# A spectral mixer beside a gated MLP: the column stage streams its tiles from DRAM, and the second half of the tokens runs as block products

## The chip, the cores and the metric

The kernel runs on one core of a Trainium2 chip. A core has TensorE (matrix products into PSUM), VectorE and ScalarE (elementwise work, and all reads of PSUM), GpSimd and SyncE (here mostly issuers of DMAs), and 16 DMA engines between DRAM and SBUF. The metric is device time in microseconds (us); lower is better.

## The reference

Two branches read the same 2048 x 576 input `x`, and a gate per token mixes them:

```python
g = sigmoid((x * gate_w).sum(-1, keepdims=True))
a = irfft2(rfft2(x) * (w_r + 1j * w_i))              # over 2048 tokens and 576 features
b = (gelu(x @ w_gate) * (x @ w_up)) @ w_down         # 576 -> 4608 -> 576, tanh form of gelu
out = g * a + (1 - g) * b
```

Everything is float32.

## The kernel before

**Precision.** Each float32 operand of a matmul is split into a high part of 12 bits and a remainder; a product is three matmuls: high x high, remainder x high, high x remainder. ScalarE makes the high copies, VectorE the remainders. The 576 features are 512 plus 64. Of the last 64 the high part and remainder are stacked along the rows, so that one matmul multiplies several of the three terms at once.

**The MLP.** The 2048 tokens are two halves of 1024, and a half has two token blocks of 512. The 4608 hidden features are 36 tiles of 128, two tiles to a block, so 18 blocks in a half. A *plain* block (`normal` L1510, `hidden` L892, `chain` L853) computes gate and up for two tiles and two token blocks: 2 x 2 x 2 chains of 14 matmuls. A *block product* (`products` L1300) gets the same from seven products instead of eight (Strassen's scheme in Winograd's form): features and tokens are halved, and seven pairs of sums of input parts (`a11`, `a12`, `s2`, `s3`, `s1`, `a22`, `s4`) and of weight parts are multiplied. `seven` (L1285) runs one such product, for gate and for up, with 7 matmuls each: six for two feature tiles of 128 and one, the seventh, for the stacked last 32 features of each feature half. `FIRST = (2, 6)` (L32): in half 0 the first 2 blocks are plain and 16 are block products, in half 1 it is 6 and 12. Each block then has 96 output matmuls of 288 columns (`down` L960, `down_mm` L935), eight groups of 12. ScalarE scales each group by 1 - g into one of four buffers `stg` (L977), and GpSimd issues a DMA that adds it to an accumulator `yd` in DRAM (L958).

**Weights of a block product.** `load` (L1237) fetches four quarters `r11, r21, r12, r22` of 128 x 768 (384 KB); the last 256 columns are the stacked tail. `prep` (L1256) is called three products ahead: VectorE takes differences of quarters (L1269), two gaps later ScalarE copies the high part (L240, and the tail with a mask at L1276), two further gaps on VectorE takes the remainder (L1279). The slots are four, used in turn. The remainders of 18 down weights are stored to DRAM in half 0 (L836) and fetched in half 1 (L829).

**Input operands of half 1.** The split inputs of the seven products of half 0 lie in `til`, `xhi`, `xlo` and `xtl`. Half 1's are made in half 0 and kept in DRAM as `kept` and `four_d` (`other_operands` L1143). During half 1's six plain blocks `til` holds the spectral tiles; after it the operands are fetched from `kept`.

**The spectral branch** is a generator (`spectral` L705): gates and forward row transforms of each half (`forward_rows` L531, `send_away` L580, which writes 16 tiles of 128 x 580 to `away` in DRAM), the column stage (`columns` L252), the last tile butterflies (`last_tiles` L450), and for each half inverse rows (`inverse_rows` L628) and the addition of g times the result to `yd` (`adds` L669). In `columns` all 16 tiles lie in `til`. For each tile: `product(0)`, a 128 x 128 complex transform in 6 matmuls on TensorE (L305), a filter on VectorE, `product(1)` back, and copies into the tile. Filter tables (`load_ww` L275, two pairs) and transform matrices (`load_cc` L271, two of each kind) are loaded two tiles or five steps ahead. `corner` (L280) regroups two quarters of a tile with DMAs of 72.5 KB.

**The order of work is written out by hand.** The program is built in TensorE's order. After every chain half, `seven` or `down`, `gap` (L742) runs: it counts, starts what was set for that count with `at(n, ...)` (n gaps later), and lets the generator go on while it has credit. Each matmul gives credit at RATE = 1.08 times its charged time (`tick` L731: 0.2265 us for 512 columns, 0.131 for 288), and each piece of VectorE work takes its charge away, the block products' own work too. `yield None` in the generator ends its turn for this gap. A block product with its output groups has 22 gaps. Each engine, and each queue of DMA issues (SyncE's `SPq`, GpSimd's, ScalarE's), takes its instructions strictly in this order, so an instruction that waits holds those behind it. In the last block, whatever the generator still has is drained with TensorE idle, ahead of the final reads of `yd` (`load_last` L997).

## Time and profile before

| | |
|---|---|
| runs | 1323.91, 1324.33, 1324.39 us; median 1324.33 |
| profiled execution | span 1323.4 us from first to last instruction; the page gives no other time for it, so 0.9 us of the median lie outside |
| TensorE busy, clock | 1317.2 us (100%), 7294 matmuls, 1.00 of full speed |
| VectorE / ScalarE / GpSimd busy | 1163.2 (88%) / 871.8 (66%) / 274.5 us (21%) |
| DMA | 247.57 MB, mean 187 GB/s; accumulating queue 45.2%, sync queue 34.1% of 16 engines' time |

Busy times of an engine are the sum of its instructions. Matmuls are pipelined, so a single matmul's duration (392 ns for 512 columns) is longer than the time it adds. A DMA share is the mean busy share of 16 engines by the time of their packets, and can pass 1 where packets overlap.

### The profile page before, as it was taken

How to read it: one execution, taken by the hardware profiler on the slowest of the kernel's cores; microseconds unless marked ns; L12 is line 12 of the kernel's file. 1: busy time of each engine (PE TensorE's matmuls, PEld its weight loads, DVE VectorE, ACT ScalarE, POOL GpSimd, SP SyncE). 2: the span in 40 equal slices, each digit the busy share in tenths (PEclk: the TensorE clock that was granted, in tenths of full speed). 3: DMA queues.
4: the chain of work that ended last, by engine and by line, in shares of the span. 5: the costliest groups of instructions: out<-in, count | busy, mean ns of one | idle time of the engine just before them, and what ended most of it. 6: DMA issues, size and time to landing. Idle time of an engine off the chain costs nothing.

```text
span 1323.4 us, 20232 instructions
## 1 busy us (share of the span) xinstructions
PE 1317.2 (100%) x7294; PEld 1166.3 (88%) x7294; DVE 1163.2 (88%) x1654; ACT 871.8 (66%) x1583; POOL 274.5 (21%) x347
## 2 busy tenths in 40 slices
PE   9999999999999999999999999999999999999998
PEld 7888888888888888888888898888888888888888
DVE  7789999978999997976889889799999879999854
ACT  5676765665657557787688888547675676676562
POOL 0011121221212212122302231211222242222331
PEclk9999999999999999999999999999999999999999
DMA  9346776797677777999989998787777897766897
GB/s 352 139 116 130 131 135 136 158 267 167 146 153 139 151 156 183 278 237 280 284 251 247 219 210 206 124 279 194 153 150 148 202 232 163 135 141 131 182 195 181
DMA packets 109221, 247.57 MB, mean 187 GB/s; under 512 B 12864, under 2 KB 18624, under 8 KB 107328
## 3 DMA queue, kind: packets, MB, share of 16 engines
q0 software_dynamic: 46560, 96.82, 45.2%
q1 hardware_dynamic: 62128, 149.01, 34.1%
q8 instruction: 57, 0.93, 0.3%
q10 hardware_dynamic: 432, 0.44, 0.1%
q14 instruction: 44, 0.36, 0.1%
HBM read 133.88 MB, written 109.95 MB: 184 GB/s over the span
## 4 chain that ended last, share of the span: by engine, by line
PE 96%; DVE 2%; DMA 1%; ACT 0%; issue 0%; SPq 0%; DVEq 0%; ACTq 0%
PE pdn L945 33%; PE pgu L1292 20%; PE px L1292 20%; PE pgu L1294 3%; PE px L1294 3%; PE pgu L861 3%; PE pgu L862 3%; PE pgu L863 3%; DMA til<-away 1%; PE pdn L305 1%; PE px L305 1%; PE px L861 1%; PE px L862 1%; PE px L863 1%; PE pgu L867 1%; PE pgu L868 1%
## 5 line engine op out<-in xcount | busy, mean ns | idle before, releaser
L958 POOL DMA_DIRECT2D yd<-stg x264 | 227.0, 865 | 937.7 <-ACT stg L977 864.3
L977 ACT ACTIVATE stg<-pdn,omg 128x576 f32<-128x576 f32 x276 | 204.4, 742 | 318.1 <-PE pdn L945 197.2
L945 PE MATMUL pdn<-dn,hb 128*128 128x288 f32 x1572 | 230.3, 294 | 0.0
L945 PEld LDWEIGHTS pdn<-dn,hb 128*128 128x128 f32 x1572 | 221.5, 188 | 8.9 <-ACT stg L977 0.4
L1279 DVE TENSOR_TENSOR gub<-low,gub 128x768 fp32r<-128x768 f32 x124 | 118.2, 954 | 9.7 <-ACT gub L1276 7.3
L1292 PE MATMUL pgu<-xhi,gub 128*128 128x512 f32 x392 | 121.6, 392 | 0.0
L240 ACT ACTIVATE gub<-low 128x512 fp32r<-128x512 f32 (+2 forms) x147 | 97.8, 666 | 23.0 <-DVE low L1269 14.5
L945 PEld LDWEIGHTS pdn<-dn,ext 128*128 128x128 f32 x672 | 100.8, 188 | 8.0
L1292 PE MATMUL pgu<-til,gub 128*128 128x512 f32 x420 | 107.5, 391 | 0.0
L945 PE MATMUL pdn<-dn,gub 128*128 128x288 f32 x672 | 106.5, 294 | 0.0
L945 PE MATMUL pdn<-dn,ext 128*128 128x288 f32 x672 | 106.5, 294 | 0.0
L945 PEld LDWEIGHTS pdn<-dn,gub 128*128 128x128 f32 x672 | 95.0, 188 | 0.0
L1292 PEld LDWEIGHTS pgu<-til,gub 128*128 128x128 f32 x420 | 76.9, 188 | 14.8 <-DVE gub L1279 0.3
L1292 PE MATMUL px<-xhi,gub 128*128 128x512 f32 x280 | 86.9, 391 | 0.0
L1292 PE MATMUL px<-til,gub 128*128 128x512 f32 x336 | 85.8, 391 | 0.0
L945 PE MATMUL pdn<-dn,hx 128*128 128x288 f32 x516 | 81.7, 294 | 0.0
L1292 PEld LDWEIGHTS pgu<-xhi,gub 128*128 128x128 f32 x392 | 70.9, 188 | 12.1
L1269 DVE TENSOR_TENSOR low<-low 128x768 f32<-128x768 f32 x81 | 77.2, 954 | 0.8
L1292 PE MATMUL pgu<-xlo,gub 128*128 128x512 f32 x196 | 76.4, 390 | 0.0
L862 PE MATMUL pgu<-xhi,gub 128*128 128x512 f32 x188 | 73.7, 392 | 0.0
L861 PE MATMUL pgu<-xhi,gub 128*128 128x512 f32 x188 | 73.7, 392 | 0.0
L863 PE MATMUL pgu<-xlo,gub 128*128 128x512 f32 x188 | 73.3, 390 | 0.0
(274 smaller groups left out, 2966.6 us busy)
## 6 DMA issues: line engine op xcount, KB each, us to landing
yd<-stg POOLq DMA_DIRECT2D x264, 288.0 KB, 5.0
low<-ws SPq DMA_DIRECT2D x94, 384.0 KB, 4.8
gub<-wd SPq DMA_DIRECT2D x56, 288.0 KB, 3.9
low<-wgu SPq DMA_DIRECT2D x13, 640.0 KB, 8.6
rows<-col POOLq DMA_DIRECT2D x32, 256.0 KB, 6.4
gub<-ws SPq DMA_DIRECT2D x18, 384.0 KB, 5.3
lo<-dn SPq DMA_DIRECT2D x18, 288.0 KB, 2.9
dn<-lo POOLq DMA_DIRECT2D x18, 288.0 KB, 5.4
```

The lines of the kernel that those rows point to most:

```text
L240: act.activation(o, i, AF.Copy)
L305: pe.matmul(v[al][:, :NK], c[:, al, q], two(x)[:, al], start=n == 0, stop=n == 2)
L861: pe.matmul(ps, w[:, 0, k, c], xhi[tb][:, k], start=k == 0, stop=False)
L862: pe.matmul(ps, w[:, 1, k, c], xhi[tb][:, k], start=False, stop=False)
L863: pe.matmul(ps, w[:, 0, k, c], xlo[tb][:, k], start=False, stop=False)
L945: pe.matmul(ps[half], h[:, l, c], d[:, q, half * HD:(half + 1) * HD], start=part == 0 and n == 0, stop=part == 1 and n == 2)
L958: pl.dma_start(yd[u], o, accum_op=ALU.add)
L977: at(n, lambda: put(u, lambda o: act.activation(o.rearrange("p (c k) -> p c k", c=2), v[:, :, 0:HD], AF.Copy, scale=omg[:, u:u + 1]), i == 0))
L1269: vec.tensor_tensor(o, p, q, ALU.subtract)
L1279: vec.tensor_tensor(w[:, 0:5:2], x, f(w[:, 1:4]), ALU.subtract)
L1292: pe.matmul(ps, l, x[:, t], start=first and t == 0 and q == 0, stop=False, skip_group_check=True)
L1294: pe.matmul(ps, w[:, 512 + P * s:512 + P * (s + 1)], xt, start=False, stop=True, skip_group_check=True)
```

## The change

1. `FIRST = 2`: only the first two blocks of half 0 are plain. Half 1 is 18 block products, without plain blocks, without its own plain weights, inputs (`xt[1]`), and without the stored down remainders (`lo`).
2. Tails of weights: a weight quarter is now 128 x 512 (256 KB). The last 64 rows go apart: `tail_piece` loads them for two blocks of four pairs (`PAIRS`), takes the differences for all seven products, splits them once, and stores the result in DRAM (`tails_d`). `prep` then fetches a tail into rows 0 to 95 of its slot with three DMAs of 32 x 256 (32 KB each) on SyncE's queue, 21 a block. The seventh matmul uses 96 rows.
3. All seven operands of half 1 are kept in DRAM (`kept`, 1280 KB each) and fetched with three DMAs each from ScalarE's queue, two gaps after half 0's last use of the same operand (`swap`).
4. The column stage no longer needs `til`: tiles are loaded from `away` four at a time into a part of `rows`, regrouped by four DMAs of 72.5 KB each (`bring`), and results are written to `gone` (`leave`). `product` uses the `pdn` PSUM buffers; the filter tables and the transform matrices have one buffer instead of two. A tile takes 6 steps instead of 5. The stage starts as soon as `other_operands` is done, in half 0, among block products.
5. `inverse_tiles` (instead of `last_tiles`) reads `gone`, does the last twiddles, and writes `home`; `inverse_rows` fetches from `home` and does the final butterfly itself (`arrive`).

The core of the diff:

```diff
-STEP = 5
-FIRST = (2, 6)
+STEP = 6
+FIRST = 2
+PAIRS = ((2, 3, 4, 5), (6, 7, 8, 9), (10, 11, 12, 13), (14, 15, 16, 17), (0, 1))
...
+        gone = dram.tile([P, 16 * SW], F32, name="gone", tag="gone")
+        home = dram.tile([P, 16 * SW], F32, name="home", tag="home")
+        kept = {n: dram.tile([P, 2560], F32, name=f"kept_{n}", tag=f"kept_{n}")
+                for n in ("a11", "a12", "s2", "s3", "s1", "a22", "s4")}
+        tails_d = [dram.tile([3 * P, 7 * 256], F32, name=f"tails{i}", tag=f"tails{i}") for i in range(len(PAIRS))]
...
+            inp = [rows[:, 7 * SW:8 * SW], wtb[:, 2 * SW:3 * SW]]
+            w0, w1 = (wtb[:, SW * i:SW * (i + 1)] for i in range(2))
...
+            def load_g(kb):
+                if kb < 16:
+                    q = SW * (kb // 4 + 4 * (kb % 4))
+                    nc.sync.dma_start(G[kb % 4], away[:, q:q + SW])
...
-                    pl.dma_start(cc(s, kb), a["col"][s, turn[kb]])
+                    for q, o in cc_parts[s]:
+                        pl.dma_start(o, a["col"][s, turn[kb]][:, q:q + o.shape[1]])
 
             def load_ww(kb):
                 if kb < 16:
+                    for c, w in enumerate((w0, w1)):
...
+            def bring(kb):
+                if kb < 16:
+                    o, i = two(inp[kb % 2]), two(G[kb % 4])
                     for c in range(2):
-                        nc.sync.dma_start(ww[kb % 2][c], a["wf"][turn[kb], c])
-
-            def corner(kb, slot, back):
-
-                if not 0 <= kb < 16:
-                    return
-                z, c = two(Z[kb]), cns[slot + kb % 2]
-                if back:
-                    copy(z[0:64, 1], c[0:64])
-                    copy(z[64:128, 0], c[64:128])
-                else:
-                    nc.sync.dma_start(c[0:64], z[64:128, 0])
-                    nc.sync.dma_start(c[64:128], z[0:64, 1])
-
-            def rest_of(l, x, h):
-                vec.tensor_tensor(l, x, f(h), ALU.subtract)
+                        for al in range(2):
+                            nc.sync.dma_start(o[64 * c:64 * c + 64, al], i[64 * al:64 * al + 64, c])
+                    at(4, lambda: load_g(kb + 4))
+
+            def leave(kb):
+                q = SW * (4 * (kb // 4) + kb % 4)
+                o, i = gone[:, q:q + SW], two(out)
+                for c in range(2):
+                    nc.sync.dma_start(o[:, NK * c:NK * (c + 1)].rearrange("(l m) k -> m l k", l=2), i[64 * c:64 * c + 64])
...
-                load_cc(d, kb + 2)
+                at(1, lambda: load_cc(d, kb + 1))
...
+                v = product(0, kb, xh, xl)
+                if was:
+                    copy(yh, vs)
+                yield from step()
...
+                if not new:
+                    bring(kb + 2)
...
+                u = product(1, kb - 1, yh, yl) if was else None
+                vec.tensor_tensor(z, z, w0, ALU.mult)
+                vec.tensor_tensor(vs, vs, w1, ALU.mult)
+                vec.tensor_tensor(z, z, vs, ALU.add)
+                vec.tensor_tensor(vs2[:, 0], zr, zi, ALU.add)
+                vec.tensor_tensor(vs2[:, 1], zr, zi, ALU.subtract)
+                at(3, lambda kb=kb: load_ww(kb + 1))
+                if new:
+                    yield from group(new)
+                    bring(kb + 2)
+                yield from step()
+                if was:
+                    copy(two(out), u[:, :, :NK])
+                    at(1, lambda kb=kb: leave(kb - 1))
...
+            def load(d):
+                if d < 4:
+                    nc.sync.dma_start(places[d % len(places)], gone[:, 4 * SW * d:4 * SW * (d + 1)])
+
+            def store(d, x):
+                nc.sync.dma_start(home.rearrange("p (e d k) -> p d e k", d=4, e=4)[:, d],
+                                  x.rearrange("p (e k) -> p e k", e=4))
...
+            for d in range(4):
+                yield from four(T[d], range(4), sp, 1)
+                if d > 1:
+                    yield from tile_twiddles(T[d - 1], d - 1, LEFT, 1, tmps)
+                if d == 0:
+                    leave(0)
+                else:
+                    tile_copies(T[d], d, LEFT, 1, tmps)
+                    if d > 1:
+                        at(1, lambda d=d: leave(d - 1))
...
+        def arrive(e):
+            B = tmp[:, 0:4 * SW].rearrange("p (t k) -> p t k", t=4)
+            yield from _butterfly(vec, lambda i: B[:, i], lambda i: B[:, i, re], lambda i: B[:, i, im],
+                                  range(4), wtb[:, 0:SW], 1, (0.76, 0.45))
+            yield from moved(lambda t, c: (spread(c, t), batch[:, t % 4, c, 0:KF]),
+                             range(4 * (e % 2), 4 * (e % 2) + 4))
+
+        def fetch(e):
+            nc.sync.dma_start(tmp[:, 0:4 * SW], home[:, 4 * SW * e:4 * SW * (e + 1)])
...
+                fetch(0)
                 yield from waits(4)
-                yield from inverse_stages()
+                yield from arrive(0)
+                at(2, lambda: fetch(1))
+                yield from waits(6)
+                yield from arrive(1)
             else:
-                yield from back_again(1)
-                yield from inverse_stages()
-            while ops.get("phase") != 1:
-                yield None
-            places = [zb[0][:, 1920:1920 + D]] + [mk(f"spare{n}", [D]) for n in range(2)]
+                yield from arrive(3)
+            yield from inverse_stages()
...
-            while not back[0] or count[0] < back[0]:
-                yield None
             yield from columns()
-            yield from last_tiles()
+            yield from inverse_tiles()
...
+        def swap(name):
+            hi, lo, tail = ops[name]
+            for o, q in ((hi, 0), (lo, 1)):
+                act.dma_start(f(o), kept[name][:, 1024 * q:1024 * (q + 1)].rearrange("p (t k) -> p t k", t=2))
+            act.dma_start(f(tail), kept[name][:, 2048:])
...
+            ring = [free_low[:, 0:TB], free_low[:, TB:2 * TB], wtb[:, 2 * TB:3 * TB],
+                    *(tmp[:, TB * i:TB * (i + 1)] for i in range(4)), zb[0][:, 1664:1664 + TB]]
...
+                        at(2, lambda n=n, h=h: nc.sync.dma_start(kept[n][:, 2048:], h))
+                    else:
+                        def store(n=n, i=i, h=h, o=o):
+                            for c, s in ((0, h), (1, o)):
+                                nc.sync.dma_start(kept[n][:, 1024 * c + TB * i:1024 * c + TB * (i + 1)], s)
+                        at(2, store)
...
+        def tail_piece(n):
+
+            def load():
+                for q, o in enumerate((raw_t[:, 0:2], raw_t[:, 3:7:3])):
+                    nc.sync.dma_start(o, a["wt"][n // 2, n % 2, q].rearrange("p (b k) -> p b k", b=2))
+
+            def total():
+                for o, p, q in ((4, 3, 0), (2, 6, 4), (3, 6, 3), (5, 1, 2)):
+                    vec.tensor_tensor(raw_t[:, o], raw_t[:, p], raw_t[:, q], ALU.subtract)
+                credit[0] -= 1.15
+
+            def high():
+                copy(high_t, raw_t)
+
+            def rest():
+                vec.tensor_tensor(fr(raw_t), raw_t, f(high_t), ALU.subtract)
+                credit[0] -= 1.1
+
+            def store():
+                d = tails_d[n // 2].rearrange("(r p) (m c k) -> r p c m k", r=3, m=7, c=2)
+                for r, x in enumerate((high_t, high_t, raw_t)):
+                    nc.sync.dma_start(d[r, :, n % 2], f(x) if r < 2 else x)
+                stored[n // 2] = n % 2
...
+                self.groups = [(0, i) for i in range(FIRST, NBLK)] + [(1, i) for i in range(NBLK)]
...
-                        credit[0] -= 0.95
-
-                w, x = (z.rearrange("p (b k) -> p b k", k=256) for z in (w, x))
+                        credit[0] -= 0.69
+
+                def tail():
+                    n, q = self.tail_at[self.groups[k][1]]
+                    assert stored[n]
+                    d = tails_d[n].rearrange("(r q p) k -> q r p k", r=3, q=4)[q, :, :, 256 * m:256 * (m + 1)]
+                    for r in range(3):
+                        nc.sync.dma_start(f(w[32 * r:32 * r + 32, 512:768]), d[r])
...
-                    copy(w[:, 1:4:2], x[:, 0:3:2])
-                    act.activation(w[:, 2], x[:, 1], AF.Copy, scale=msk[:, 1:2])
+                    copy(v[:, 1:4:2], x)
 
                 def rest_of():
-                    vec.tensor_tensor(w[:, 0:5:2], x, f(w[:, 1:4]), ALU.subtract)
-                    credit[0] -= 1.0
+                    vec.tensor_tensor(v[:, 0:5:4], x, f(v[:, 1:4:2]), ALU.subtract)
+                    credit[0] -= 0.69
...
+                seq(("b", k, m), (lead, total), (lead + c, high), (lead + c, tail), (lead + d, rest_of))
...
-                pe.matmul(ps, w[:, 512 + P * s:512 + P * (s + 1)], xt, start=False, stop=True, skip_group_check=True)
+                pe.matmul(ps, w[0:96, 512 + P * s:512 + P * (s + 1)], xt[0:96], start=False, stop=True,
+                          skip_group_check=True)
...
+            if 0 < k <= 2 * len(PAIRS) - 2:
+                for n, fn in zip((1, 8, 10, 13, 15), tail_piece(k + 1)):
+                    at(n, fn)
...
+                if turn:
+                    assert ops["kept"]
+                    at(2, lambda name=name: swap(name))
...
+        b = Block()
+        for i in range(FIRST):
+            for tb in range(2):
+                normal(i, tb, b)
+        for k in range(len(b.groups)):
+            if k == len(b.groups) - 1:
+                assert ops["half"]
+                for u in range(8):
+                    nc.sync.dma_start(a["y"][u], yd[u])
+            products(b, k)
```

685 lines of the change are left out of this document (268 added, 417 removed).

## The prediction

> **What bounds the kernel now.** I read the page first (busy times, slices, chain), then a table of stretches whose borders come from the chain of waits in order of time, then the waits of TensorE.
>
> ```profile
> span 1323.4 us, 20232 instructions
> ...
> PE 1317.2 (100%) x7294; PEld 1166.3 (88%) x7294; DVE 1163.2 (88%) x1654; ACT 871.8 (66%) x1583; POOL 274.5 (21%) x347
> ...
> PE 96%; DVE 2%; DMA 1%; ACT 0%; issue 0%; SPq 0%; DVEq 0%; ACTq 0%
> ```
> ```profile
> 168.30 3.16 PE pdn L945 x24
> ...
> 203.31 3.16 PE pdn L945 x24
> ...
> 845.05 3.16 PE pdn L945 x24
> ...
> 883.23 3.16 PE pdn L945 x24
> ```
> ```profile
> 0.00:35.00 35.00, 33.55 (x151) 27.84 (x152) 27.71 (x49) 20.91 (x38) 3.11 (x10) 1.00 0.95 351
> 140.00:175.00 35.00, 35.00 (x196) 31.01 (x195) 33.47 (x52) 24.79 (x50) 6.86 (x8) 1.00 0.69 130
> 623.00:658.00 35.00, 35.00 (x207) 31.59 (x206) 28.75 (x47) 22.36 (x35) 11.69 (x15) 1.00 1.07 291
> 655.00:830.00 175.00, 174.30 (x994) 155.90 (x993) 157.14 (x266) 143.22 (x265) 35.29 (x51) 1.00 0.89 226
> 1302.00:1323.40 21.40, 17.36 (x117) 16.35 (x115) 12.02 (x19) 2.55 (x5) 0.28 (x1) 1.00 0.61 183
> ```
> ```profile
> PE px L305 <- DVE rows L293: 0.7, 1, 0.7
> ```
>
> The columns of a stretch are its length, the busy time of TensorE, weight load, VectorE, ScalarE and GpSimd, the granted clock, the DMA share and GB/s. TensorE is busy 1317.2 of 1323.4 us at clock 1.00. Its 6.2 idle us are 1.45 at the start, 4.04 at the end, and 0.70 at one wait early in the column stage. So the time is a count of matmuls, and an edit pays only by removing some or by making TensorE wait.
>
> The 24 output matmuls that close a block return every 35.01 us among block products (168.30 to 203.31) and after 38.18 us where a plain block was done (845.05 to 883.23). Both kinds run 96 output matmuls; a block product has 7 x 2 x 7 = 98 gate/up matmuls, a plain block 2 x 2 x 2 x 14 = 112. So 14 gate/up matmuls are 3.17 us and 12 output matmuls 3.16 / 2 = 1.58, and one product with its output set is 4.75.
>
> **What TensorE loses.** The second half had 6 plain blocks of 18 (FIRST = (2, 6)) and now has none: 6 x (38.18 - 35.01) = **19.0 us off**. The column stage keeps 16 x 2 x 6 = 192 matmuls. The seventh matmul of each group has 96 rows instead of 128; no row of before has such a shape, and its nearest rows are the 128-row ones, which stream 512 columns either way. I take no gain and no loss. The 0.70 us wait was on the split of the first column tile; a new prologue with 11 gaps of waiting replaces it, so **0.7 off**.
>
> **What VectorE and ScalarE gain and lose.**
>
> ```profile
> L1279 DVE TENSOR_TENSOR gub<-low,gub 128x768 fp32r<-128x768 f32 x124 | 118.2, 954 | 9.7 <-ACT gub L1276 7.3 <-PE px L1294 2.3
> L1276 ACT ACTIVATE gub<-low,msk 128x256 fp32r<-128x256 f32 x124 | 61.8, 498 | 0.0
> L1269 DVE TENSOR_TENSOR low<-low 128x768 f32<-128x768 f32 x81 | 77.2, 954 | 0.8
> L1312 DVE TENSOR_TENSOR xraw<-xraw 128x512 f32<-128x512 f32 x56 | 38.4, 686 | 9.6 <-ACT xraw L1316 9.5
> L833 DVE TENSOR_TENSOR dn<-gub,dn 128x576 fp32r<-128x576 f32 x38 | 28.6, 752 | 0.0
> L833 DVE TENSOR_TENSOR gub<-low,gub 128x1280 fp32r<-128x1280 f32 x13 | 19.3, 1487 | 0.2 <-ACT gub L240 0.2
> ```
>
> A block product makes 7 remainders and 4 differences of weights. They shrink from 768 columns (954 ns) to 512 (686): 28 x 11 x 0.954 = 294 us become 34 x 11 x 0.686 = 257. Six more blocks add 24 sums (+16), 12 remainders of plain weights go (12 x 1.487 = -18), the 18 down remainders that were stored and fetched are computed again (18 x 0.752 = +14), and ten tail pieces cost by the planner's charges 2.25 each (+22). VectorE stays near 1160 us, 89% of a shorter span: no new bound. ScalarE sheds the 498 ns copy seven times a block, 3.5 us. All of this lies beside TensorE and is worth nothing while every remainder is ready: a block weight is prepared three products (14.2 us) ahead, finished 4 gaps later (22 gaps to 35.01 us, so 1.59 each), which leaves 8 us.
>
> **What the DMAs gain.**
>
> ```profile
> yd<-stg POOLq DMA_DIRECT2D x264, 288.0 KB, 5.0
> low<-ws SPq DMA_DIRECT2D x94, 384.0 KB, 4.8
> rows<-col POOLq DMA_DIRECT2D x32, 256.0 KB, 6.4
> ...
> low<-wf SPq DMA_DIRECT2D x16, 290.0 KB, 6.4
> ...
> ext<-til SPq DMA_DIRECT2D x48, 72.5 KB, 5.6
> ```
> ```profile
> L289 SPq DMA_DIRECT2D ext<-til x24: 461/467/1459, 647.7 to 821.5; - x24
> ```
>
> The last figure of an issue row is the median time to landing; the other row has the min/median/max ns of one issue on SyncE.
>
> Each block now fetches its tail weights in 21 DMAs of 32 KB, 21 x 0.47 = 10 us of SyncE's queue. They are issued about 3 gaps into a lead of 14 us, so landing in 5.6 us leaves 3 to 4 us for whatever waits ahead of them on SyncE. Bytes per block: 8 x 288 + 4 x 256 + 2 x 288 + 21 x 32 KB = 4.7 MB, 134 GB/s, against 130 measured.
>
> The column stage moves, per tile: filter 580 KB, tile from DRAM 290, regrouping 290, two matrices 512, result 290: 2.0 MB, where before it was 1.4 MB. It is 16 x 6 steps of one gap plus about 19 gaps for the three groups made inside: 115 x 1.59 + 26 us of column matmuls = 209 us, 155 GB/s. Together 290 GB/s for 209 us; before, the stage ran at 226 GB/s and share 0.89.
>
> New waits. The filter tables are single: loaded 3 gaps after the filter, wanted 3 gaps (4.8 us) on, landing 6.4 plus an issue. VectorE stands about 2 us per tile, with block remainders queued behind it; their 8 us hide this until landing nears 11 us. The matrices are single too: product to product is 6 gaps and two products, 11 us, the load is issued one gap in, so 8 to 9 us are there for a landing of 6.4, behind the accumulates on GpSimd's queue. This wait is TensorE's own and nothing hides what exceeds it. Regrouping has 7 gaps, but 4 (6.4 us) right after a group, against 4 issues and 5.6 us: ScalarE is late by about 1 us three times.
>
> **The turn** from half 0 to half 1: 21 DMAs on ScalarE's queue bring 7 x 1280 KB = 9.2 MB in one block, each operand wanted one block later. The last block of half 0 runs from about 592 to 627 us (the closing matmuls at 168.30, 12 periods on), and by the planner's charges the columns start near 586, so they collide. Over the 57 us in which all must land, 57 x 290 GB/s = 16.5 MB + 9.2 = 25.7 MB. Bounds: the fastest stretch above moved 351 GB/s, 20.0 MB in 57 us, so 5.7 MB or 16 us are over; at the 291 of the fastest stretch that had accumulates in it, 9.1 MB or 31 us. Against that stand the four output buffers (4 x 4.75 - 5.0 = 14 us) and the weights, about 11 us of allowance. That gives 5 to 20 us; below nothing is excluded, since no matmul goes. I take the lower end, **+5**, because the stretch at 291 cost TensorE nothing (35.00 of 35.00), though its share was 1.07: a share above 1 counts overlapping packets, and is no wall.
>
> **Sum.** 1323.4 - 19.0 - 0.7 + 5 = 1308.7. The runs' median, 1324.3, lies 0.9 over the profiled span: **1309.6 us**; its own range 1304 (no stall) to 1318.
>
> **Rivals.**
>
> *The DMAs bound the column stage (slower side).* Place: first column product to the landing of the turn's operands and the last tile. Need: 209 us x 290 GB/s + 9.2 = 69.8 MB. At 284 GB/s, the mean of the 70 us in which before's column stage opens (row below), that takes 246 us: 37 more than planned, less 11: +26, 1304.6 + 26 = **1331**. It decides from about 292 GB/s down, where the stall reaches 20 us and eats the gain. For it: no row with accumulates held more than 291, and landing rose there.
>
> ```profile
> DMA packets 9373, 19.87 MB, mean 284 GB/s; under 512 B 1019, under 2 KB 1787, under 8 KB 9368
> ...
> til<-away SPq DMA_DIRECT2D x8, 580.0 KB, 9.7
> yd<-stg POOLq DMA_DIRECT2D x12, 288.0 KB, 7.7
> ```
>
> Against it: in those 70 us TensorE lost 0.7. The Trainium skill (DMA: Bandwidth & Descriptors, Issuing engines are not separate DMA queues) says that DMAs issued from the scalar, sync and gpsimd engines run on the same 16 DMA engines and interleave, so a third queue adds no bandwidth. By that rule the turn pays in full and this rival is the outcome; the rise of the accumulates' landing from 5.0 to 7.7 us beside the sync queue's load agrees with it.
>
> *The spectral chain does not end in time.* The last block drains what is left of it with TensorE idle.
>
> ```profile
> L567 DVE TENSOR_TENSOR rows<-tmp x8: 740/794/854, 1060.9 to 1083.4; 128x289 f32<-128x289 f32 x8
> ```
> ```profile
> 1257.55 0.82 DVE L683 TENSOR_SCALAR gub<-rows,gs 128x576 f32<-128x576 f32 x1
> ```
> ```profile
> 1299.84 7.60 SPq L999 DMA_DIRECT2D stg<-yd  x4
> ```
>
> Before, the last scaling came at 1257.6, 42 us ahead of the final reads (1299.84). A block now leaves the spectral side 1.08 x 34.8 - 17.4 = 20.1 planner units instead of 16.9 to 18.4, so 78.5 units of inverse row stages take about 141 us instead of 154 (1083.4 to the scalings from 1237 on). Adding the stages up (columns 586 to 801, tiles to 863, rows to 1048 and 1251) puts the last scaling near 1272, the final reads at 1281: 9 us of room on a sum uncertain by 20. An overrun of 20 us leaves 12 units to drain: +12 on 1304.6 + 5, **1322**.
>
> *The tails come late.* If SyncE is held 4 us longer than above (a store that waits for VectorE ahead of them), every block pays: 0.1 us per product x 238 = 24 us, **1333**. Against: SyncE has 56 issues x 0.47 = 26 us per 35 us in the column stage, 13 elsewhere, so at most the column stage pays.
>
> **How the numbers follow.** Forecast 0.57, DMA-bound columns 0.26, late chain 0.12, late tails 0.05. A change under 0.2% (2.6 us) can't be told from none. Faster: nearly all of the first, a third of the second (stalls up to 17 us) and half of the third, 0.70; same: 0.08; slower: 0.22. The range starts at the floor, 1304, and reaches past 1331 to 1334, where the rest of the DMA case, about 0.12, and late tails beyond it are left out.
>
> **What would show it.** Right: 7210 matmuls, closing matmuls 35.01 us apart outside the columns, TensorE idle about 11 us, all of the increase between 590 and 800 us, and a DMA share at 1.0 there. TensorE waits named after the matrix loads or the operands' swap show the turn; waits spread over all 16 tiles show the DMA rival; idle TensorE ahead of the final reads shows the late chain; waits of weight loads on tail DMAs in every block the last one. The forecast is wrong if the column stage is stretched by more than 12 us, or if the closing matmuls stand further apart than 35.01 us in the pure block stages.

## The result and the profile after

The changed kernel takes **1388.97 us** (median; 1385.02 to 1389.90) against 1324.31 (1323.91 to 1324.39): ratio 1.0483, 95% interval 1.0468 to 1.0498. It is 64.7 us slower, where 14.7 us faster was forecast. Ratios and intervals use fast executions alone; the only slow one (1360.5 us at a clock of 0.92) belongs to the run g1 below. The profiled execution took 1389.90 us, with this page:

```profile
span 1388.1 us, 21347 instructions
...
PE 1330.7 (96%) x7210; PEld 1168.4 (84%) x7210; DVE 1150.5 (83%) x1814; ACT 802.4 (58%) x1395; POOL 274.8 (20%) x345
...
PEclk9999999999999999998899999999999999999999
```

The 84 matmuls are gone (7294 to 7210), and VectorE is no fuller. But TensorE is idle for 1388.1 - 1330.7 = 57.4 us instead of 6.2, and its fewer matmuls take *more* busy time. The chain of waits in the stage of block products alone tells one reason:

```profile
1001.52 3.18 PE pdn L891 x24
...
1036.83 3.18 PE pdn L891 x24
...
1072.14 3.18 PE pdn L891 x24
```

The closing matmuls stand 35.31 us apart. Before it was 35.01. Over 34 block products 0.30 us each make 10.2 us.

So the 64.7 us are: matmuls -19.0, longer blocks +10.2, idle time 57.4 - 6.2 = +51.2, and the rest of the growth of busy time, 1330.7 - (1317.2 - 19.0 + 10.2) = +22.3. The table of stretches shows where the last two lie (length; busy time of TensorE, weight load, VectorE, ScalarE, GpSimd, each with its number of instructions in brackets; clock, DMA share, GB/s):

```profile
560.00:980.00 420.00, 378.62 (x2030) 329.93 (x2029) 307.87 (x521) 258.92 (x456) 86.59 (x118) 0.96 0.93 242
...
560.00:595.00 35.00, 28.06 (x143) 23.55 (x142) 20.76 (x33) 28.16 (x50) 7.72 (x10) 0.95 0.92 252
630.00:665.00 35.00, 23.74 (x111) 20.30 (x110) 18.84 (x33) 17.36 (x30) 6.29 (x9) 0.85 0.95 277
665.00:700.00 35.00, 27.69 (x147) 24.63 (x146) 22.39 (x38) 18.01 (x32) 5.99 (x8) 0.85 0.97 262
770.00:805.00 35.00, 30.96 (x167) 26.83 (x166) 24.66 (x44) 21.98 (x39) 5.86 (x9) 0.95 0.93 253
980.00:1330.00 350.00, 350.00 (x1928) 309.45 (x1927) 320.83 (x473) 200.21 (x344) 76.68 (x89) 1.00 0.79 155
1330.00:1388.10 58.10, 46.17 (x272) 42.17 (x270) 31.19 (x48) 15.69 (x26) 15.44 (x17) 0.94 0.87 186
```

From 980 to 1330 TensorE is full at clock 1.00. Of the 57.4 idle us 41.4 lie between 560 and 980, worst from 630 to 700, and 11.9 in the last 58. Where TensorE stalls, its granted clock falls too. And these are its waits (us in total, times, longest):

```profile
PE pdn L891 <- ACT stg L923: 27.2, 9, 7.3
PE pdn L891 <- DVE low L956: 8.0, 2, 7.1
PE pgu L1286 <- ACT xraw L235: 7.0, 1, 7.0
PE pdn L307 <- DMA tmp<-col: 2.9, 3, 1.3
```

It hardly ever waits for a DMA itself (the longest group, on the transform matrices, has 2.9 us). It waits for ScalarE to empty the PSUM buffers of the output groups (L923): what was late lies further back.

### The profile page after: what moved, and what is told of

It is laid out like the page before. It is cut to its first block, busy times and chain, and to the rows that moved or that the text cites. A ratio compares the mean times of both kernels' runs of the same rounds, so it can differ in the third digit from the quotient of the medians.

```text
span 1388.1 us, 21347 instructions
## 1 busy us (share of the span) xinstructions
PE 1330.7 (96%) x7210; PEld 1168.4 (84%) x7210; DVE 1150.5 (83%) x1814; ACT 802.4 (58%) x1395; POOL 274.8 (20%) x345
## 5 line engine op out<-in xcount | busy, mean ns | idle before, releaser
L923 ACT ACTIVATE stg<-pdn,omg 128x576 f32<-128x576 f32 x276 | 204.3, 742 | 380.6 <-PE pdn L891 245.2
L891 PE MATMUL pdn<-dn,ext 128*128 128x288 f32 x816 | 134.4, 301 | 22.4 <-ACT stg L923 14.3
L1286 PE MATMUL pgu<-xhi,gub 128*128 128x512 f32 x480 | 152.5, 399 | 1.0 <-DVE gl L1311 1.0
L1286 PE MATMUL pgu<-til,gub 128*128 128x512 f32 x516 | 135.3, 398 | 7.0 <-ACT xraw L235 7.0
L235 ACT ACTIVATE gub<-low 128x512 fp32r<-128x512 f32 (+1 forms) x163 | 100.8, 620 | 31.3 <-DVE low L1257 17.6
L1273 DVE TENSOR_TENSOR gub<-low,gub 128x512 fp32r<-128x512 f32 x151 | 103.4, 684 | 3.4 <-ACT gub L235 3.4
L1286 PE MATMUL pgu<-xlo,gub 128*128 128x512 f32 x240 | 94.7, 395 | 0.0
L1286 PEld LDWEIGHTS px<-til,gub 128*128 128x128 f32 x396 | 72.6, 188 | 14.0
L1286 PEld LDWEIGHTS px<-xhi,gub 128*128 128x128 f32 x344 | 62.2, 188 | 13.1 <-DVE xraw L1328 1.5
L93 DVE TENSOR_TENSOR rows<-rows 128x1280 f32<-128x1280 f32 (+1 forms) x57 | 69.5, 1219 | 0.8
L1288 PE MATMUL pgu<-til,gub 96*128 96x512 f32 x172 | 68.3, 397 | 0.3 <-DMA gub<-tails 0.3
```

Of the source, the lines that this page charges most:

```text
L93: eng.tensor_tensor(o, p, q, op)
L235: act.activation(o, i, AF.Copy)
L891: pe.matmul(ps[half], h[:, l, c], d[:, q, half * HD:(half + 1) * HD], start=part == 0 and n == 0, stop=part == 1 and n == 2)
L923: at(n, lambda: put(u, lambda o: act.activation(o.rearrange("p (c k) -> p c k", c=2), v[:, :, 0:HD], AF.Copy, scale=omg[:, u:u + 1]), i == 0))
L1273: vec.tensor_tensor(v[:, 0:5:4], x, f(v[:, 1:4:2]), ALU.subtract)
L1286: pe.matmul(ps, l, x[:, t], start=first and t == 0 and q == 0, stop=False, skip_group_check=True)
```

## The experiments

Below, 1389 is the changed kernel. Single executions are compared with it, and its own spread over 5 us, so smaller differences are not read; g1 to g3 were timed in three rounds.

### The turn, the tails, the bytes

```diff
 e1_no_turn
-                    at(2, lambda name=name: swap(name))
 e2_tails_once
+                once = [(lead + c, tail)] if 7 * k + m < 4 else []
+                seq(("b", k, m), (lead, total), (lead + c, high), *once, (lead + d, rest_of))
 e3_few_bytes  (swap, load_ww, load_cc)
+                n = SW if kb == 0 else SW // 4
```

> The changed kernel without the 21 fetches of the turn on ScalarE's queue: half 1's block products use half 0's operands, so the second half's MLP is computed from the wrong inputs; everything else stands. Theory T (the turn's 9.2 MB stall the two blocks around it): the worst stretch, 630 to 700 us, where TensorE was busy 51 of 70 us at a clock of 0.85, becomes like its neighbours (64 of 70), about 1365 us. Theory Q (SyncE's queue: the column stage's own fetches stand behind tail fetches that wait for TensorE): no more than 10 us are gained, 1380 or above. Theory B (too many bytes for the DMA engines): 9.2 MB at 270 GB/s are 34 us, so about 1355.

> The changed kernel, where only the first four products fetch a tail into their slot and all later products reuse what lies there: 234 of 238 times three DMAs of 32 KB are gone from SyncE's queue, and the tail rows of the result are wrong. Theory Q: the 351 us in which SyncE's queue stood at these fetches go, the column stage's fetches are issued in time, and the idle 57 us of TensorE shrink to under 25, the clock with them: about 1335 us. Theory T: the stage keeps its stalls, 1385. Theory B: 0.69 MB less per block over some 10 blocks is 7 MB or 25 us: about 1362.

> The changed kernel with the same DMAs in the same order, but the turn's, the filter tables' and the transform matrices' (after the first tile) move a quarter of their columns: about 7 + 12 = 19 MB less between 590 and 890 us, and the operands of half 1 and the filters are wrong. Theory B: 19 MB at 270 GB/s are 70 us of DMA time, so the stalls of the stage are nearly gone, 1335 us or less. Theory Q: the order of the queue is what it was, so at most 15 us are gained, 1375. Theory T says what the run without the turn says, about 1365.

Measured: without the turn **1365.6**, with tails fetched once **1371.4**, with a quarter of the bytes **1356.4**. The turn costs 23 us, as theory T had it, but T alone promised 1385 for the run without tail fetches, and 14 us less came. Theory B promised 1335 or less for a quarter of the bytes and falls as the whole story; theory Q promised 1335 for the tails and falls too.

The trace of the changed kernel shows how the turn reached TensorE. ScalarE issues these fetches itself, in its own order. An issue stood until an earlier DMA had landed, and ScalarE's copies stood behind the issue. This is the end of one operand's three fetches, and TensorE right after it:

```profile
671.38 0.33 ACTq L1018 DMA_DIRECT2D til<-kept_a  x1
671.76 0.63 ACT L235 ACTIVATE gub<-xraw 128x512 fp32r<-128x512 f32 x1 [7.92 <-DMA til<-kept_s]
...
672.81 0.72 ACT L923 ACTIVATE stg<-pdn,omg 128x576 f32<-128x576 f32 x1
```
```profile
673.59 3.25 PE L891 MATMUL pdn<-dn,hb 128*128 128x288 f32 x12 [7.31 <-ACT stg L923]
```

Four times between 618 and 672 us ScalarE was idle around such issues, for 7.1, 7.4, 6.6 and 7.9 us, 29.0 in all. TensorE's waits of 1.6, 7.0, 4.2 and 7.3 us end 1 to 5 us after them, and none of its waits names a fetch of the turn. With a quarter of the bytes ScalarE's idle time at these issues is 11.8 us, without tail fetches 15.4, and TensorE's busy time from 630 to 700 rises from 51.4 us to 65.6 and 64.6 (67.6 without the turn). So two things make the price together: the DMAs landed late, and the engine that empties PSUM stood for them. No run separates the two; the same fetches from another engine's queue were not tried.

In the run without the turn something else is left, which comes back about every 70 us, four tiles. This is the timeline of VectorE, ScalarE and TensorE there (start, duration, engine, instruction; in brackets the idle time before it and what ended it):

```profile
707.84 0.76 DVE L354 TENSOR_TENSOR rows<-rows,wtb 128x580 f32<-128x580 f32 x1 [4.48 <-DMA wtb<-wf]
709.67 0.76 DVE L355 TENSOR_TENSOR rows<-rows,wtb 128x580 f32<-128x580 f32 x1 [1.07 <-DMA wtb<-wf]
```
```profile
712.93 0.69 ACT L427 ACTIVATE low<-rows 128x580 f32<-128x580 f32 x1 [6.87 <-DVE rows L441]
...
714.19 0.72 ACT L923 ACTIVATE stg<-pdn,omg 128x576 f32<-128x576 f32 x1
```
```profile
714.97 1.81 PE L891 MATMUL pdn<-dn,ext 128*128 128x288 f32 x6 [6.33 <-ACT stg L923]
```

Read it downwards. The filter table lands 4.5 us after VectorE wants it. The regrouping step of every fourth tile has a copy on ScalarE (L427) that needs VectorE's twiddle (L441), which stands behind the filter. ScalarE takes its work in order, so the copy waits 6.9 us, and the emptying of an output group (L923) behind it waits along. TensorE has no PSUM buffer and stands 6.3 us. Four links, each in order, turn a late table into a stall.

### The price of a stall

```diff
 e4_stalls, in the kernel before, ahead of four output groups (n = 6, 12, 20, 30)
+                for n in (stall, 0):
+                    pe.matmul(v[0:112, 0, 0:112], spare_s, spare_s, start=True, stop=True)
+                    for _ in range(n):
+                        pl.memset(f(spare_s), 0.0)
```

> The kernel before, with four stalls of TensorE put into block products of the first half, two blocks apart: a small matmul reads a spare tile of 112 columns, GpSimd clears that tile 6, 12, 20 and 30 times after it (about 0.25 us each by the rows of the fills of before), and a second small matmul reads it again; results are unaffected. So TensorE stands about 1.5, 3, 5 and 7.5 us, 17 us in all. Theory C (the granted clock falls after a stall of some us and takes time to come back): the windows behind the longer stalls show a clock under 1.00 and matmuls that take longer, and the time grows by more than the stalls: 1324 + 17 + 5 to 15. Rival (the clock fell for another reason in the changed kernel, as its load of DMAs): the clock stays at 1.00 and the time is 1341.

Measured: 1358.9, that is +34 us. TensorE's wait, and the windows around the third stall:

```profile
PE pdn L971 <- POOL hb L973: 25.0, 4, 9.4
```

```profile
398.00:400.00 2.00, 0.00 (x0) 0.00 (x0) 0.00 (x0) 0.00 (x0) 1.54 (x9) 0.50 0.02 1
400.00:402.00 2.00, 1.57 (x7) 1.58 (x8) 0.00 (x0) 0.00 (x0) 0.31 (x2) 0.50 0.00 0
...
404.00:406.00 2.00, 2.00 (x8) 1.60 (x7) 0.76 (x2) 1.73 (x3) 0.85 (x1) 0.80 0.00 0
406.00:408.00 2.00, 2.00 (x12) 1.72 (x11) 2.00 (x3) 1.90 (x4) 0.00 (x0) 1.00 0.85 103
```

The four waits were 3.5, 5.1, 7.0 and 9.4 us, longer than meant. When TensorE resumes at 400.4 after the third, the clock is 0.50 and stays there to about 405. Behind the shortest stall, which ended at 243.2, it fell about a microsecond later, from 244.4 to 247.8:

```profile
242.00:244.00 2.00, 0.83 (x6) 0.83 (x7) 0.59 (x1) 0.00 (x0) 0.89 (x5) 1.00 1.08 267
244.00:246.00 2.00, 2.00 (x11) 1.91 (x10) 0.00 (x0) 0.27 (x1) 0.00 (x0) 0.59 0.31 55
246.00:248.00 2.00, 2.00 (x7) 1.59 (x6) 0.98 (x2) 1.51 (x3) 0.85 (x1) 0.55 0.00 0
```

Busy time grew by 1326.7 - 1317.2 = 9.5 us, about **2.4 us for each of the four stalls** on average. Busy time times the missing share of the clock, summed over windows of half a microsecond, gives 1.7, 3.0, 2.2 and 2.2 us for them, so it does not grow with the length. Theory C stands. The Trainium skill (TensorE: Matmul & The Clock Gate, Part 1: The HAM clock gate) says that an idle window of about 3.4 us sends TensorE to half clock, and that it has to be busy for about as long before the clock is back; the rows of these four stalls agree with both.

In the changed kernel the same sum finds eight drops of the clock and 17.1 of the 22.3 us; the rest is not settled. Two of the eight stand behind shorter waits, of 1.86 us (at 76.9) and of 2.50 us, so 3.5 us is no floor, and by the measurement 3.4 us of idle time is not needed either:

```profile
579.67 1.22 PE L1286 MATMUL pgu<-xhi,slot 128*128 128x512 f32 x2 [2.50 <-ACT px L235]
```
```profile
580.00:582.00 2.00, 2.00 (x6) 1.54 (x6) 0.71 (x2) 1.97 (x4) 0.88 (x1) 0.50 0.00 0
```

### Spacing, rate, and the place of the tails

```diff
 e5_apart
+                    if i == 2:
+                        yield None
...
                     bring(kb + 2)
+                    yield from waits(4)
 e6_rate
-RATE = 1.08
+RATE = 1.14
 e7_one_dma
-                    for r in range(3):
-                        nc.sync.dma_start(f(w[32 * r:32 * r + 32, 512:768]), d[r])
+                    nc.sync.dma_start(f(w[0:96, 512:768]), d)
 e9_tail_later
-                seq(("b", k, m), (lead, total), (lead + c, high), (lead + c, tail), (lead + d, rest_of))
+                seq(("b", k, m), (lead, total), (lead + c, high), (lead + d, rest_of), (lead + d, tail))
 e11_rate_late
                 yield from columns()
+                rate[0] = 1.14
```

> The changed kernel with two local edits that are read in separate windows. (1) In the making of half 1's operands one gap is put after each of the seven last splits, so that ScalarE's copies of 32 rows (0.63 us each, 8 in a row in the run without the turn) no longer stand in one batch ahead of the release of the PSUM buffers. (2) After each of the three groups inside the column stage four more gaps pass (6.4 us each). Theory P (steps packed too tightly for in-order engines): TensorE's busy time in 560 to 595 rises from 28 us to above 32, and of the losses that come back every 70 us in the runs without the turn and with fewer bytes (28 to 33 of 35 us busy in the windows at 700, 770 and 840) most go; the chain starts 19 gaps (30 us) later, so that the drain at the end grows by up to 20 us. Rival (these losses are DMA latency in a loaded queue, whatever the spacing): the windows stay as they are.

Measured: 1395.8. The first window mends, and the loss moves into the next:

```profile
560.00:595.00 35.00, 32.83 (x171) 28.58 (x170) 20.63 (x33) 27.40 (x48) 9.39 (x12) 0.95 1.02 270
595.00:630.00 35.00, 26.70 (x140) 23.19 (x140) 19.48 (x33) 12.88 (x24) 4.87 (x6) 0.89 0.89 219
```

TensorE's two longest waits on ScalarE in the first window (2.39 and 2.50 us) shrink to one of 1.97, so ScalarE's batch of copies is part of the stall before 595. How large a part stays open: 28.06 busy became 32.83, but the run f4 below has 31.12 with the same edit, and runs without it (at RATE 1.08 up to there) 27.35 to 31.11. What is behind the window is late anyway. Four gaps behind each group don't restore the stage, and the later start is paid at the end.

> The changed kernel with RATE 1.14 instead of 1.08: the generator gets 5% more credit per matmul, so that the spectral chain runs earlier. Theory L (the last block drains what is left of a late chain): the loss behind 1360 us (TensorE busy 16 of 28 us at a clock of 0.88) shrinks to the 4 to 5 us of the kernel before, 10 us in all, about 1379 if the column stage stays as it was. Rival (the end is set by the accumulates that stand behind each other, not by the chain's lateness): the end stays, and denser steps make the column stage worse, 1389 or more.

Measured: 1390.4. The end is mended, and the stage of block products, full before, loses 11.5 us, with VectorE busier there (415.22 us; 405.94 in the changed kernel):

```profile
105.00:560.00 455.00, 443.45 (x2398) 389.86 (x2397) 415.22 (x645) 266.75 (x465) 87.13 (x107) 0.98 0.89 206
1330.50:1388.60 58.10, 54.22 (x337) 49.90 (x335) 23.74 (x37) 21.60 (x35) 10.28 (x12) 1.00 0.83 199
```

> The changed kernel, with RATE 1.14 from the end of the column stage on and 1.08 before it. Theory L (the loss behind 1360 us is the late chain alone): TensorE is busy 20 of 25 us or more behind 1360, as in the run with 1.14 throughout, without that run's loss of 11.5 us between 105 and 560: 1389 - 12 = 1377. Rival (the earlier chain pushes VectorE's block work aside in the inverse stages, so the gain is given back there): 980 to 1295 falls under 310 of 315, 1385 or more.

Measured: **1380.1**, 9 us less, and 980 to 1295 stays full (315.00 of 315). Its last 58.1 us:

```profile
1320.20:1378.30 58.10, 54.16 (x337) 49.82 (x335) 27.57 (x43) 21.28 (x35) 15.09 (x18) 0.98 0.93 235
```

Idle time there falls from 11.9 to 3.9 us, about the 4.0 of the kernel before. Theory L stands: the loss at the end is the late chain, and an earlier one costs the inverse stages nothing.

> The changed kernel, where a product's tail is fetched by one DMA of 96 rows instead of three of 32: the same bytes, 476 DMA instructions fewer on SyncE's queue; the wait for TensorE's last read of the slot stays. Fetching no tails saved 18 us (1371 against 1389). Theory Qn (it is the number of issues, 0.47 us each, 7 us per block less): 12 us or more are gained, 1377. Theory Qw (it is the wait for TensorE ahead of the other fetches) and theory B (it is the bytes): 1385 to 1389.

> The changed kernel with a product's three tail fetches issued two gaps (3.2 us) later, behind the remainder of its weights; bytes and number of DMAs are unchanged. On SyncE's queue these fetches waited 351 us in 138 waits of 2.5 us each for TensorE's last read of the slot. Theory Qw (what stands behind that wait on SyncE's queue comes late, and that starves ScalarE and VectorE in the column stage): the waits shrink to under 100 us, and 10 to 18 us are gained, about 1373. Theory B (bytes and landing times set the stalls): within 5 us of 1389. If the tails now come too late themselves, waits of TensorE on tails appear in the pure block stages, and the time is above 1395.

Measured: 1401.2 with one DMA instead of three, 1397.7 with the tails two gaps later. Both are slower. The waits of SyncE's queue at the tail fetches, in the changed kernel and then in e9, and TensorE's new waits in e7 and in e9:

```profile
SPq L1265 <- PE pgu L1288: 180.2, 69, 5.1
SPq L1265 <- PE px L1288: 171.2, 69, 5.0
```
```profile
SPq L1265 <- PE pgu L1288: 108.0, 43, 5.1
SPq L1265 <- PE px L1288: 106.6, 50, 5.1
```
```profile
PE pgu L1287 <- DMA gub<-tails: 6.7, 5, 2.2
```
```profile
PE pgu L1288 <- DMA gub<-tails: 6.5, 2, 3.9
PE px L1288 <- DMA slot<-tails: 4.5, 1, 4.5
```

The waits on the queue fell from 351 to 215 us, not under 100 as expected, and nothing was gained. But in both runs the tails themselves came late, which for e9 was the third case of its expectation: TensorE waited 11.0 us for them, at 519, 600 and 925 us. So neither run supports theory Qn or Qw, and neither rules them out, because the late tails cover what might have been gained. Where the 18 us without tail fetches come from can be narrowed: TensorE gains 13.3 us from 560 to 980, and 13.1 of them lie between 630 and 700, at the turn, where ScalarE stood 15.4 instead of 29.0 us. Whether the bytes of the tails or their place in the queue did it was not tried apart.

### Turn and columns apart, and all reliefs together

```diff
 e10_late_columns  (columns)
+            while not ops.get("turned"):
+                yield None
...
-                    at(2, lambda name=name: swap(name))
+                    at(2, lambda name=name: [swap(name), ops.update(turned=name == "s4")])
```

> The changed kernel, where the column stage does not start before the last fetch of the turn has been issued; nothing is left out. Theory T+C (turn and columns collide, as the prediction's term for the turn had it; either alone is covered): the block of the turn is nearly full, TensorE busy 33 of 35 us or more in each window until the columns start near 645 us, and the stage behind it looks as in the run without the turn, 28 to 35 of 35. Rival (the turn alone is too much for its block: its 9.2 MB beside the blocks' 134 GB/s and the stores of the operands): a window before the columns' start shows 30 or less. The chain ends about 40 to 55 us later either way, and the last block drains it with TensorE idle: 1389 - 24 + 30 to 50, so 1395 to 1415.

Measured: 1406.6. The first matmul of the columns comes at 682.2, and the window of the turn before it reads:

```profile
630.00:665.00 35.00, 26.44 (x128) 22.39 (x127) 15.89 (x25) 11.53 (x21) 6.84 (x9) 0.85 1.06 333
```

The rival is right: the turn without a matmul of the columns takes 8.6 us of TensorE and its clock beside (the first four tiles and the first filter pair are fetched in this window too, 1.8 MB). ScalarE stood at its fetches here as well, for 7.2, 5.9 and 4.8 us from 635 to 659. The window moves 333 GB/s at a share of 1.06. That agrees with the rule that the prediction named from the Trainium skill (DMA: Bandwidth & Descriptors, Issuing engines are not separate DMA queues): fetches on ScalarE's queue were not free beside SyncE's. The rule does not tell of the other half, that ScalarE's own work stood behind them.

> The three reliefs together: no fetches of the turn, tails fetched only into the first four slots, and filter tables and matrices (after the first tile) with a quarter of their columns; so half 1's operands, the tails and the filters are wrong. If the causes add up (24 us for the turn, 18 for the tails, and 33 for the bytes less what of it is the turn's, 9 to 15), about 1389 - 24 - 18 - 12 = 1335, and what is left above 1309 is packing of the steps and the late chain at the end. If all three only relieve one shared queue and its wall, the sum is less: 1350.

Measured: 1348.2. The reliefs don't add up: 41 us instead of 54, as the second case of the expectation had it (1350). With most of the extra traffic gone the stage from 560 to 980 still loses 13 us idle:

```profile
560.00:980.00 420.00, 406.86 (x2246) 359.02 (x2245) 341.33 (x571) 277.58 (x488) 93.72 (x127) 0.99 0.81 183
```

### The filter tables

```diff
 f1_tables_aside; f2_aside_no_turn is the same without swap
+                        o = w if kb == 0 else aside[:, SW * (2 * kb + c):SW * (2 * kb + c + 1)]
-                        nc.sync.dma_start(w, a["wf"][turn[kb], c])
+                        nc.sync.dma_start(o, a["wf"][turn[kb], c])
 f3_ww_early
-                at(3, lambda kb=kb: load_ww(kb + 1))
+                at(1, lambda kb=kb: load_ww(kb + 1))
 f4_mended: f3 with e11's rate and e5's first edit
```

> The changed kernel, where the filter tables after the first tile's are copied to a place in DRAM that nobody reads, at the same point of SyncE's queue and with the same bytes read; every tile is filtered with the first tile's table, so the spectral result is wrong. No instruction of VectorE waits for a table any more (16.6 and 3.5 us in all before). Theory F (a late table holds VectorE, VectorE holds the group's copy on ScalarE, and the copy of the output group behind it on ScalarE's queue comes late, so that TensorE has no PSUM buffer): 20 us of VectorE's waits cause about 20 us of TensorE's stalls with the clock behind them, 1389 - 15 to 20 = 1370 or so. Rival (the traffic as such): the same bytes, so 1385 or more.

> The same with the fetches of the turn left out too (half 1 uses half 0's operands): beside the run without the turn, 1365.6. Theory F: the losses that came back every 70 us there (TensorE busy 28.3, 29.9 and 32.7 of 35 us in the windows at 700, 770 and 840, each with a wait of VectorE of 3.6 to 4.9 us for a table) shrink to 1 to 3 us each, and the time to about 1350. Rival: the windows stay, 1362 or more.

> The changed kernel with the filter tables of the next tile issued one gap after the filter instead of three, that is 3.2 us earlier; nothing is left out. Theory F: three of the 4 to 6 us by which VectorE waits for a table are gone each time, waits of VectorE on tables fall from 20 to under 8 us, and the time to about 1376. Rival: SyncE now waits for the filter at that point and the other fetches of the tile come late instead, 1385 or more.

> Three edits together, nothing left out: filter tables two gaps earlier, a gap after each of the last seven splits of half 1's operands, and RATE 1.14 behind the column stage. If their gains add up (about 12, 5 and 9 us), 1363; if the stalls only move to the next late fetch, 1375 or more, the 9 us of the late chain and little else. Either way above 1324: the turn's 24 us, which none of the three touches, is more than the 19 us that the block products save.

Measured: **1372.8, 1355.0, 1374.6, 1373.9**. At equal bytes, but with nobody waiting, 16 us go; in the run without the turn 11 us; and issuing the tables 3.2 us earlier, with nothing left out, gains 14. VectorE's wait for tables in the changed kernel, and TensorE's first wait in f3, beside 27.2 us above:

```profile
DVE rows L354 <- DMA wtb<-wf: 16.6, 4, 6.6
```
```profile
PE pdn L891 <- ACT stg L923: 16.4, 8, 4.2
```

Theory F stands, most clearly in the run without the turn: its windows at 700, 770 and 840 rise from 28.27, 29.92 and 32.73 us busy to 34.11, 31.97 and 34.72, and 9.1 of the 9.4 us that TensorE gains from 560 to 980 lie behind 700. In the other two a part lies elsewhere. The changed kernel's four waits for tables come from 726 to 866 us, but of the 12.3 (f1) and 10.6 us (f3) that TensorE gains from 560 to 980 only 7.6 and 3.6 lie behind 700. What moved the windows ahead of it was not tried. The fourth run gains nothing over the third. It lost more between 595 and 630 (27.74 of 35 busy, against 32.64 in f3), as e5 did, which eats what the end gives.

### The 96 rows

```diff
 g1_rows96, in the kernel before
-                pe.matmul(ps, w[:, 512 + P * s:512 + P * (s + 1)], xt, start=False, stop=True, skip_group_check=True)
+                pe.matmul(ps, w[0:96, 512 + P * s:512 + P * (s + 1)], xt[0:96], start=False, stop=True, skip_group_check=True)
 g2_rows128, in the changed kernel
+                for w in self.slots:
+                    pl.memset(f(w[96:128, 512:768]), 0.0)
...
-                pe.matmul(ps, w[0:96, 512 + P * s:512 + P * (s + 1)], xt[0:96], start=False, stop=True,
+                pe.matmul(ps, w[:, 512 + P * s:512 + P * (s + 1)], xt, start=False, stop=True,
 g3_together: g2 with f3's tables and e11's rate
```

> The kernel before with one edit: the seventh matmul of each group takes rows 0 to 95 instead of all 128, so that the fourth stacked group of 32 rows is left out of the sum. In the changed kernel the 24 closing matmuls stand 35.31 us apart in the pure block stage (1001.52, 1036.83, 1072.14), in the kernel before 35.01: 0.30 us per block that the prediction did not have. Theory R (a matmul of 96 rows among matmuls of 128 costs about 0.30 / 14 = 21 ns more): 28 block products, so 1324.3 + 28 x 0.30 = 1332.7, and closing matmuls 35.31 apart. Rival, the prediction's step (rows cost nothing, and the 0.30 us have another source, such as the DMAs of the tails): 1324.3 and 35.01.

> The changed kernel with 128 rows in the seventh matmul: rows 96 to 127 of the four slots' tails are filled with zeros once, so nothing is left out. Theory R: 34 block products, 34 x 0.30 = 10.2 us less, about 1379, and closing matmuls 35.01 us apart in the pure stage. Rival: 1389 and 35.31.

> The changed kernel with the three mends that are known by their own runs, nothing left out: 128 rows in the seventh matmul (10 us by theory R), filter tables issued two gaps earlier (14 us), RATE 1.14 behind the column stage (9 us). If they add up, 1389 - 33 = 1356; if the rate's gain is not there again because the tables already brought the chain forward, 1362; by the rival on the rows, 1366 or more. Above 1324 in each case.

Measured: g1 **1334.7** (ratio to the kernel before 1.0075, interval 1.0059 to 1.0092), g2 **1378.9** (1.0413, 1.0397 to 1.0428), g3 **1370.5** (1.0343, 1.0326 to 1.0361). The closing matmuls of g1, then of g2:

```profile
133.85 3.19 PE pdn L945 x24
169.19 3.19 PE pdn L945 x24
```
```profile
992.52 3.16 PE pdn L891 x24
1027.55 3.16 PE pdn L891 x24
```

Theory R stands from both sides: 96 rows in the kernel before make its blocks 35.34 us long (+10 us), 128 rows in the changed one make them 35.03 again (-10 us). The three mends of g3 would sum to 33 us and gave 18.5. The end is full there (54.19 of the last 58.1 us, as in e11), but from 560 to 980 it is not better than the changed kernel with 128 rows (380.92 busy against 383.02 in g2; f3 had 389.20). VectorE's waits for tables were mostly gone (6.4 us, where g2 has 21.3), but TensorE now waited 4.1 us for a tail and still 20.5 us for ScalarE's emptying of PSUM (27.4 in g2). So the gain of the earlier tables was not there when the whole stage lay a little differently. No version tried is faster than the kernel before. The turn alone, at 23 us, outweighs the 19 us that the matmuls give, so a faster one would need another way to fetch the operands, for instance not from the queue of the engine that empties PSUM; that was not tried.

## Why the prediction was wrong

**What held.** 7210 matmuls; 84 fewer are worth 19 us. VectorE is no bound. The pure block stages are full. Most of the idle time lies around the turn and the columns, as announced (560 to 980 us, where the prediction had 590 to 800), and it is worst at the turn. Late tails as a rival did not decide in the way it was put: TensorE's waits name no tail among the large ones. Fetching them still cost 18 us, most of it at the turn.

**Rows cost 0: wrong, +10.2 us.** The nearest rows stream the same 512 columns, and the recorded duration of the seventh matmul hardly shows it (395 ns, 389 before, in the rows below). The prediction's own test, closing matmuls further apart than 35.01, caught it. For an instruction of the engine that sets the time, a shape that no row shows is an unknown with two ends, not a zero.

**The turn, +5: mis-sized, 23, and by another path.** The bounds were 5 to 20 and the lower end was taken, because a stretch at 291 GB/s had cost nothing. The working held about 11 us of allowance against late operands, from the four output buffers and the weights, and looked for waits of TensorE on the operands themselves. No such wait came. ScalarE, which has to empty those buffers, stood at its own fetches for 29 us, so the allowance was not there; even without a matmul of the columns the turn's window lost 8.6 us plus clock. The kind of the DMA rival was partly right here (0.26, 1331), its place was not: outside the turn a quarter of the tables' bytes gave only 9 us more.

**The filter tables' wait, hidden: wrong, 11 to 16 us.** The prediction named the wait (about 2 us, single tables) and the cover (8 us of slack in VectorE's block remainders). The wait was 1.6 to 6.6 us where it came, four times in 16 tiles, and the cover was the wrong one: the way to TensorE did not lead over remainders, but over ScalarE's queue, where a group's copy waits for VectorE with the emptying of an output group behind it. The prediction had seen these three groups and put "ScalarE late by about 1 us" there, without asking what stands behind it.

**The chain ends late: it did.** This rival (0.12, +12) came true besides, at 9 us. The columns began at 608 instead of 586 and took about 280 us (to 888) instead of 209. In the working of this rival, 78.5 units at 20.1 a block are 137 us, not 141; that gives 4 us more room and changes no bound.

**The clock: not priced at all, 17 of 22 us.** Each stall was counted at its length. In the changed kernel eight waits of 1.9 us and more came with a lower clock, at 2.1 us of busy time each. The gains of the runs above contain their share of it.

The forecast with the terms at their measured sizes (15 for the tables) is 1309.6 + 10 + 18 + 15 + 9 = 1362. The 27 us to 1389 that are left are not settled: the batch of copies before 595 is one part (up to 5 us in its window), the tails at the turn may be another, and f4 and g3 show that stalls of the stage move when one of them is mended.

## What to carry to other kernels

Follow a late transfer through every in-order queue up to the bounding engine, and ask at each engine what stands *behind* the instruction that waits; slack in one consumer covers nothing of another. The same holds for the issue of a transfer: an engine that issues it in its own order does nothing else while the issue waits. When the bounding engine has been full at full clock, a stall of a few us costs more than its length (about 2 us more here), so price it with the clock. Where the time is a count of matmuls, a new shape of matmul is measured first: 20 ns each was half the gain here.

## What was not expected of the hardware

A matmul of 96 rows among matmuls of 128 costs 21 to 24 ns (0.30 us over 14 in a block of the changed kernel, 0.33 over 14 in g1), of which its own duration shows 6 (3 in g1; min/median/max ns; the kernel before, then the changed one):

```profile
L1294 PE MATMUL pgu<-til,gub x136: 387/389/395, 76.9 to 1303.1; 128*128 128x512 f32 x136
```
```profile
L1288 PE MATMUL pgu<-til,gub x172: 391/395/628, 81.5 to 1357.3; 96*128 96x512 f32 x172
```

A closing group of 24, which holds none but follows one, takes 3.18 to 3.19 us instead of 3.16. Why was not tried.

And one DMA of 96 rows instead of three of 32 rows made the kernel 12 us slower at equal bytes. The median issue on SyncE's queue took 711 ns against 3 x 419, so it is not the issue that grew; TensorE waited 8.5 us for late tails there, and the rest is open (the changed kernel, then e7):

```profile
L1265 SPq DMA_DIRECT2D slot<-tails x177: 302/419/1632, 78.4 to 1328.5; - x177
```
```profile
L1264 SPq DMA_DIRECT2D slot<-tails x59: 681/711/2616, 78.6 to 1337.4; - x59
```
